# Setup and first step of a fused convolution + MoE kernel: loads on three queues, four scratch sets, eight plain products, order by arrival

## The chip, the cores and the metric

One core of one Trainium2 chip. The metric is the time of one launch in device microseconds (us). The changed kernel was timed beside the kernel before in the same rounds; the experiments ran in three groups, on three chips, each again beside the kernel before. A ratio compares the fast runs of two kernels in the same rounds; it is not quite the ratio of the medians quoted beside it.

## The reference

```python
# x (8, 4096, 192) f32, weight (8, 7) f32; moe_w_in (192, 2048) f64, moe_w_out (2048, 192) f64
w = softmax(weight, axis=-1)                       # one 7-tap kernel per head of 24 channels
x_pad = concat([zeros((B, 6, D)), x], axis=1)      # causal
out[b, s, h, :] = sum_k w[h, k] * x_pad[b, s + k, h, :]
h = out.reshape(32768, 192) @ w_in
g = h * (1 / (1 + exp(-1.702 * h)))
return (g @ w_out).astype(float32)
```

## The kernel before

The work is 64 steps of 512 tokens. In each step TensorE (PE) computes first products (f by w_in, into PSUM accumulators) for two units a and b. ScalarE (ACT) applies gelu and VectorE (DVE) adds partial results. PE then computes second products (g by w_out). Both products use a Strassen-like scheme: seven 2x2 block products in place of eight, fed by sums of the blocks (`sums_w_out` for w_out, `sum_g` for g). Two steps share one x block. DVE prepares the next block's convolution f in small lots (`work(n)`) between other work, and at the end of a preparation a DMA copies f crosswise between the partition halves (`cross`). In the code of a step, p1 to p7 are first products on PE; `seed`, `keep2` and `keep3` are copies out of PSUM on ACT (into `sums` and `u`); `add12` and `add22` are additions on DVE; h11 to h22 are gelus on ACT, which write g.

Before step 0 the kernel loads x and the float64 weights and rounds the weights to float32 by integer work, piece by piece. A piece is split by two DVE and four ACT instructions and rounded by three or four on DVE. There are four pieces of w_in and four of w_out. x block 0 is convolved on PE itself, by 42 products with diagonal matrices. In the traces DVE and PE work through their lists in the order of the program: in e2 below, transposes that could start at 9.32 us (e6) stood on DVE until 13.84, 4.5 us behind work that was not ready, and in e6 a part of the convolution stood on PE behind a product that waited 2.57 us.

The loads and the diagonal matrices:

```python
    load_x(0)                                   # 8 transfers on SyncE's queue, 640-byte rows
    ...
    for i in range(NW):                         # 4 pieces of w_in, each two 64-partition halves
        piece = raw[:, i, :].rearrange("p (k f) -> p k f", k=NC)
        for h in range(2):
            nc.sync.dma_start(out=piece[halves[h], :, :], in_=w_in_v[i // 2, i % 2, h])
    ...
    for c in range(NC):
        for k in range(K):
            vec.tensor_scalar_mul(diag[:, c, k, :], ident, cw[:, c, k : k + 1])
    new_f(0)
    for c in range(NC):
        transpose_x(0, c)
```

The seven-product form at the end of each step. Its second product needs a sum of w_out (S4), so in step 0 it waits for the whole rounding of w_out:

```python
        p1 = product2(ra, 0, A11, B11)
        act.copy(u1, p1)
        for i in range(4):
            last.sum_g(i)
        p3 = product2(rb, 0, S4, B22)
        ...
```

The lots of work in steps 0 and 1. In step 1, `output` takes only part of the queue and the rest, with the crossing, is drained after it:

```python
        work(6) if s else setup0()
        ...
        if s == 0:
            setup1()
        else:
            work(None if s % 2 and s > 1 else 4)
        ...
        output(s, b, work)
        if s == 1:
            work()
```

## Time and profile before

| | before |
|---|---|
| median of the first 3 runs | 2518.4 us (2517.91 to 2520.95) |
| span of the profiled run | 2520.6 us |
| convolution on PE starts | 11.36 us |
| first second product of step 0 | 59.78 us |
| first product of step 1 | 92.67 us |
| first product of step 2 | 141.47 us |
| first u copy of step 2 on ACT ("step-2 mark") | 168.22 us |

From step 2's mark on, nothing differs between the kernels of this document, so a kernel is judged best by when it reaches that mark. The floor is 38.1 us a step, and 0.1 to 1.1 us are added in single steps that differ from run to run. Differences of some us between single runs, and of 1 or 2 us between medians, can come from there.

The prediction shows PE's waits and the stretches. Three lines more are needed for the start. First the DVE timeline (start, duration, then engine, line, operation and operands; in brackets the idle time before it and what ended it):

```profile
6.42 4.20 DVE L521 TENSOR_SCALAR diag<-ident,cw 128x128 f32<-128x128 f32 x21
10.54 2.09 DVE L296 STREAM_TRANSPOSE xt<-xin 128x576 f32<-128x576 f32 x3
```

The PE timeline at the same place:

```profile
11.36 18.30 PE L527 MATMUL slot<-xt,diag 128*128 128x512 f32 x42 [1.56 <-DVE xt L296]
```

The transposes start right behind the 21 diagonals, with no wait for a DMA: DVE sets the start of the convolution, and x has landed earlier (its last packet ended at 8.5 us; in e6, with the same load, the transposes could start at 9.3).

### The profile page before, as it was taken

How to read it: one execution, taken by the hardware profiler on the slowest of the kernel's cores; microseconds unless marked ns; L12 is line 12 of the kernel's file. 1: busy time of each engine (PE TensorE's matmuls, PEld its weight loads, DVE VectorE, ACT ScalarE, POOL GpSimd, SP SyncE). 2: the span in 40 equal slices, each digit the busy share in tenths (PEclk: the TensorE clock that was granted, in tenths of full speed). 3: DMA queues.
4: the chain of work that ended last, by engine and by line, in shares of the span. 5: the costliest groups of instructions: out<-in, count | busy, mean ns of one | idle time of the engine just before them, and what ended most of it. 6: DMA issues, size and time to landing. Idle time of an engine off the chain costs nothing.

```text
span 2520.6 us, 114341 instructions
## 1 busy us (share of the span) xinstructions
PE 2478.5 (98%) x54336; PEld 2303.3 (91%) x54336; DVE 1714.2 (68%) x2370; ACT 952.5 (38%) x1060; POOL 4.8 (0%) x20
## 2 busy tenths in 40 slices
PE   8889999999999999999999999999999999999998
PEld 5779999999999999999999999999999999999998
DVE  7856667666667666667666676666676666677654
ACT  6224334334334334334343343343343343343342
POOL 0000000000000000000000000000000000000000
PEclk9999999999999999999999999999999999999999
DMA  7122212212212222122122122122122222121110
GB/s 165 32 56 53 57 31 54 57 34 55 55 31 57 44 47 57 42 44 56 39 51 57 33 52 58 36 54 56 28 58 47 43 57 49 38 57 39 28 34 15
DMA packets 197603, 123.43 MB, mean 49 GB/s; under 512 B 115984, under 2 KB 191248, under 8 KB 193168
## 3 DMA queue, kind: packets, MB, share of 16 engines
q1 hardware_dynamic: 197120, 116.13, 21.9%
q8 instruction: 424, 6.95, 1.1%
q14 instruction: 43, 0.35, 0.0%
q10 hardware_dynamic: 16, 0.00, 0.0%
HBM read 53.15 MB, written 25.17 MB: 31 GB/s over the span
## 4 chain that ended last, share of the span: by engine, by line
PE 96%; DVE 1%; ACT 1%; DMA 1%; issue 0%; SPq 0%; DVEq 0%; ACTq 0%
PE slot L350 30%; PE slot L455 30%; PE sums L350 18%; PE slot L445 17%; PE slot L527 0%; DVE g L439 0%; ACT g L373 0%; DMA f<-f 0%; DMA xin<-in_x_dram 0%; ACT u L390 0%; DVE xt L296 0%; ACT f L198 0%; SPq L102 0%; ACT f L197 0%; ACT f L195 0%
## 5 line engine op out<-in xcount | busy, mean ns | idle before, releaser
L455 PE MATMUL slot<-g,w_out_s 128*32 128x64 f32 x21504 | 1219.6, 219 | 1.1 <-issue 0.8
L445 PE MATMUL slot<-g,w_out_s 128*32 128x192 f32 x21504 | 1209.6, 330 | 10.4 <-DVE w_out_s L257 9.9
L455 PEld LDWEIGHTS slot<-g,w_out_s 128*32 128x32 f32 x21504 | 1205.9, 110 | 2.7 <-issue 1.9
L350 PE MATMUL slot<-f,w_in_s 64*128 64x256 f32 x7168 | 843.9, 378 | 11.5 <-DMA f<-f 10.4
L350 PEld LDWEIGHTS slot<-f,w_in_s 64*128 64x128 f32 x7168 | 691.7, 188 | 100.5 <-DMA f<-f 11.2
L439 DVE TENSOR_TENSOR g<-g 128x1024 f32<-128x1024 f32 x512 | 609.5, 1222 | 191.9 <-ACT g L373 187.5
L445 PEld LDWEIGHTS slot<-g,w_out_s 128*32 128x32 f32 x21504 | 629.5, 108 | 34.2 <-issue 23.4
L350 PE MATMUL sums<-f,w_in_s 64*128 64x256 f32 x4096 | 515.1, 380 | 5.8 <-ACT sums L383 3.0
L390 ACT COPY u<-sums 128x1024 f32<-128x1024 f32 x128 | 129.5, 1012 | 1029.6 <-PE sums L350 1029.6
L350 PEld LDWEIGHTS sums<-f,w_in_s 64*128 64x128 f32 x4096 | 392.3, 187 | 56.7 <-ACT sums L383 3.7
L313 DVE SCALAR_TENSOR_TENSOR f<-xt,cw,f 128x512 f32<-128x512 f32 x558 | 417.5, 748 | 14.2
L373 ACT ACTIVATE g<-u 128x1024 f32<-128x1024 f32 x256 | 269.7, 1054 | 14.2 <-DVE u L430 14.1
L430 DVE TENSOR_TENSOR u<-u,slot 128x1024 f32<-128x1024 f32 x128 | 155.9, 1218 | 68.6 <-PE slot L350 68.6
L420 DVE TENSOR_TENSOR u<-u,slot 128x1024 f32<-128x1024 f32 x128 | 155.7, 1216 | 68.4 <-ACT u L403 65.5
L493 DVE TENSOR_TENSOR u<-u,slot 128x192 f32<-128x192 f32 x64 | 22.7, 355 | 247.7 <-PE slot L455 247.7
L403 ACT COPY u<-sums 128x1024 f32<-128x1024 f32 x128 | 129.6, 1012 | 133.7 <-PE sums L350 133.7
L373 ACT ACTIVATE g<-sums 128x1024 f32<-128x1024 f32 x128 | 130.6, 1020 | 94.7 <-PE sums L350 94.7
L373 ACT ACTIVATE g<-slot 128x1024 f32<-128x1024 f32 x128 | 131.5, 1027 | 45.0 <-PE slot L350 45.0
L383 ACT COPY sums<-slot 128x1024 f32<-128x1024 f32 x128 | 128.8, 1006 | 27.9 <-PE slot L350 25.8
L489 DVE TENSOR_TENSOR u<-u,slot 128x192 f32<-128x192 f32 x64 | 22.7, 354 | 99.6 <-PE slot L455 99.6
L483 ACT COPY u<-slot 128x192 f32<-128x192 f32 x64 | 20.4, 319 | 159.0 <-PE slot L455 159.0
L473 DVE STREAM_TRANSPOSE osb<-u 128x192 f32<-128x192 f32 x192 | 72.3, 376 | 4.4
(57 smaller groups left out, 417.5 us busy)
## 6 DMA issues: line engine op xcount, KB each, us to landing
xin<-in_x_dram SPq DMA_DIRECT2D x240, 180.0 KB, 4.5
f<-f SPq DMA_DIRECT2D x62, 576.0 KB, 4.8
out_dram<-osb SPq DMA_DIRECT2D x384, 48.0 KB, 1.7
out_dram<-osb SPq DMA_DIRECT2D x384, 16.0 KB, 1.5
g<-in_moe_w_in_dram SPq DMA_DIRECT2D x8, 384.0 KB, 9.4
g<-in_moe_w_out_dram SPq DMA_DIRECT2D x4, 768.0 KB, 5.1
xin<-in_x_dram SPq DMA_DIRECT2D x16, 160.0 KB, 3.2
f<-f SPq DMA_DIRECT2D x2, 256.0 KB, 3.4
```

The lines of the kernel that those rows point to most:

```text
L313: vec.scalar_tensor_tensor(out=dst, in0=src, scalar=tap, in1=dst, op0=ALU.mult, op1=ALU.add)
L350: nc.tensor.matmul(slot[:, h, j * T : (j + 1) * T], w_in_s[halves[h], u, a, j * P : (j + 1) * P], f[halves[h], 0 if h == o else 1, b, :], ...
L373: act.activation(g[:, b, j : j + NK // NU, :].rearrange("p f t -> p (f t)"), src.rearrange("p h n -> p (h n)"), AF.Gelu_apprx_sigmoid,)
L383: act.copy(sums, self.x)
L390: act.copy(self.u2, sums)
L403: act.copy(self.u3, sums)
L420: vec.tensor_add(self.u3, self.u3, self.z)
L430: vec.tensor_add(self.u2, self.u2, self.z)
L439: vec.tensor_sub(v[dst], v[a], v[b])
L445: nc.tensor.matmul(dst[c * Q : (c + 1) * Q, :], w_out_s[:, a, j, c * Q : (c + 1) * Q], g[:, b, j, 0:TA], start=(first and j == 0), stop=(j ...
L455: nc.tensor.matmul(dst[3 * Q :, c * TB : (c + 1) * TB], w_out_s[:, a, j, c * Q : (c + 1) * Q], g[:, b, j, TA:T], start=(first and j == 0 a ...
L473: vec.transpose(osb[:, n, :, m * Q : (m + 1) * Q], src.rearrange("p (j t) -> p j t", t=Q),)
```

## The change

The intent: start sooner, remove the wait for sums of w_out in step 0, and let nothing wait for the crossing at step 2. Its core:

```diff
-    load_x(0)
-    for i in range(NW): ... nc.sync.dma_start(...)        # all of w_in behind x, one queue
+    load_w_in(0, act)            # piece 0 on ScalarE's queue
+    load_x(0)                    # x on SyncE's
+    load_w_in(2, nc.sync)        # piece 2 behind it
     ...
+    load_w_in(1, nc.gpsimd)      # pieces 1 and 3 on GpSimd's
+    load_w_in(3, nc.gpsimd)
@@ scratch: 2 sets -> 4 (two in f, one in the x tile, one in diag)
@@ diagonals: 7 on DVE, 14 on ACT
-            vec.tensor_scalar_mul(diag[:, c, k, :], ident, cw[:, c, k : k + 1])
+            if c == 0:
+                vec.tensor_scalar_mul(diag[:, c, k, :], ident, cw[:, c, k : k + 1])
+            else:
+                act.mul(diag[:, c, k, :], ident, cw[:, c, k : k + 1])
     new_f(0)
+    split_piece(0)               # DVE: now ahead of the transposes
+    splits()
     for c in range(NC):
         transpose_x(0, c)
@@ step 0 unrolled by hand as first_step(), p1 between the convolution's parts; its end:
+        todo.extend(prepare(1))
+        for k in range(2):
+            for n in range(2):
+                for m in range(2):
+                    src = product2((b.x, b.z)[n], m, ..., first=(k == 0))   # eight plain products
+                    if k == 1:
+                        if (n, m) == (0, 0):
+                            work(5)
+                            sums_w_out()
+                        work(3)
+                        vec.transpose(osb[:, n, :, m * Q : (m + 1) * Q], ...)   # "turn"
@@ step 1: the rest of block 1's preparation is drained before add12, not after output
-            work(None if s % 2 and s > 1 else 4)
+        work(None if s % 2 else 4)
-        if s == 1:
-            work()
```

(Cut: the scratch sets' addresses, the order of step 0's first products, the loads of w_out moved to GpSimd's queue.) "Slot" is a PSUM tile of two halves, called banks here; `m` chooses the bank and `n` the slot.

More of the change, by code (lines that the diff above doesn't have):

```diff
@@ L145, with scratch @@
     raw = raw.rearrange("p (i n) -> p i n", i=NW)
-    tmp = f_pool.tile([P, 2, NB, T], F32, name="f")
-    tmp = tmp.rearrange("p o b t -> p (o b t)").bitcast(U32).rearrange("p (i n) -> p i n", i=6)
-    w8 = consts.tile([H, K], F32)
-    act.dma_start(out=w8, in_=weight)
-    load_x(0)
+    diag = consts.tile([P, NC, K, P], F32)
+    assert min(NC * K * P, 2 * NJ * XW) >= 3 * PIECE
+    def scratch(flat):
+        return [flat[:, j * PIECE : (j + 1) * PIECE].bitcast(U32) for j in range(3)]
+    tmp = f_pool.tile([P, 2, NB, T], F32, name="f").rearrange("p o b t -> p (o b t)")
+    sets = [
+        scratch(tmp),
+        scratch(tmp[:, 3 * PIECE :]),
+        None,
+        scratch(diag.rearrange("p c k q -> p (c k q)")),
+    ]
+    SET = (0, 1, 2, 0, 1, 3, 0, 1)
     w_in_v = moe_w_in.bitcast(U32).rearrange(
@@ L157, with load_w_in @@
     w_out_v = moe_w_out.bitcast(U32).rearrange("(c p) d -> p c d", p=P)
-    for i in range(NW):
+    def load_w_in(i, queue):
         piece = raw[:, i, :].rearrange("p (k f) -> p k f", k=NC)
         for h in range(2):
-            nc.sync.dma_start(out=piece[halves[h], :, :], in_=w_in_v[i // 2, i % 2, h])
+            queue.dma_start(out=piece[halves[h], :, :], in_=w_in_v[i // 2, i % 2, h])
+    w8 = consts.tile([H, K], F32)
+    act.dma_start(out=w8, in_=weight)
+    load_w_in(0, act)
+    load_x(0)
+    load_w_in(2, nc.sync)
     sel = consts.tile([H, NC, P], F32)
@@ L183 @@
         nc.gpsimd.memset(bias[:, i : i + 1], b)
+    load_w_in(1, nc.gpsimd)
+    load_w_in(3, nc.gpsimd)
     def words(i):
         w = raw[:, i % NW, :].rearrange("p (n w) -> p n w", w=2)
-        return (w[:, :, 0], w[:, :, 1]) + tuple(tmp[:, 3 * (i % 2) + j, :] for j in range(3))
+        return (w[:, :, 0], w[:, :, 1]) + tuple(sets[SET[i]])
     def split_piece(i):
@@ L194, in split_piece, with splits @@
         vec.tensor_scalar(e, hi, 20, 0x7FF, op0=ALU.logical_shift_right, op1=ALU.bitwise_and)
-        act.activation(l.bitcast(F32), lo, AF.Copy, scale=2.0**-32)
-        act.activation(e.bitcast(F32), e, AF.Relu, bias=bias[:, 0:1])
-        act.activation(e.bitcast(F32), e.bitcast(F32), AF.Relu, bias=bias[:, 1:2], scale=-1.0)
-        act.activation(
-            e, e.bitcast(F32), AF.Identity, bias=bias[:, 2:3], scale=-(2.0**23)
-        )
+        ef = e.bitcast(F32)
+        acts.extend(
+            [
+                lambda: act.activation(l.bitcast(F32), lo, AF.Copy, scale=2.0**-32),
+                lambda: act.activation(ef, e, AF.Relu, bias=bias[:, 0:1]),
+                lambda: act.activation(ef, ef, AF.Relu, bias=bias[:, 1:2], scale=-1.0),
+                lambda: act.activation(
+                    e, ef, AF.Identity, bias=bias[:, 2:3], scale=-(2.0**23)
+                ),
+            ]
+        )
+    acts = []
+    def splits(n=4):
+        for _ in range(n):
+            acts.pop(0)()
     def round_piece(i, dsts):
@@ L233, in load_w_out @@
     def load_w_out(i):
-        nc.sync.dma_start(
+        nc.gpsimd.dma_start(
             out=raw[:, i, :].rearrange("p (c d) -> p c d", c=CW),
@@ L241, in round_w_out @@
         round_piece(
-            i,
+            NW + i,
             [
@@ L501, in output, with store @@
         turn(1, 0, u3)
+        store(s, osb)
+    def store(s, osb):
         big, odd = divmod(s, 2)
@@ L515, in output, with work, first_conv @@
                 )
-    diag = consts.tile([P, NC, K, P], F32)
+    todo = []
+    def work(n=None):
+        for _ in range(len(todo) if n is None else min(n, len(todo))):
+            todo.pop(0)()
     for c in range(NC):
         for k in range(K):
-            vec.tensor_scalar_mul(diag[:, c, k, :], ident, cw[:, c, k : k + 1])
+            if c == 0:
+                vec.tensor_scalar_mul(diag[:, c, k, :], ident, cw[:, c, k : k + 1])
+            else:
+                act.mul(diag[:, c, k, :], ident, cw[:, c, k : k + 1])
     new_f(0)
+    split_piece(0)
+    splits()
     for c in range(NC):
         transpose_x(0, c)
-    for c in range(NC):
+    xs = xin_pool.tile([P, 2, NJ, XW], F32, name="xin")
+    sets[2] = scratch(xs.rearrange("p n j d -> p (n j d)"))
+    conv_out = [slots[1][:, 0, :], slots[2][:, 0, :], slots[1][:, 1, :]]
+    def first_conv(c):
         for k in range(K):
             nc.tensor.matmul(
-                slots[c][:, 0, :],
+                conv_out[c],
                 diag[:, c, k, :],
@@ L536, in take_conv @@
         vec.tensor_copy(
-            fs[0][:, 0, 2 * c : 2 * c + 2, :].rearrange("p n t -> p (n t)"), slots[c][:, 0, :]
+            fs[0][:, 0, 2 * c : 2 * c + 2, :].rearrange("p n t -> p (n t)"), conv_out[c]
         )
-    split_piece(0)
-    take_conv(0)
-    split_piece(1)
-    round_w_in(0)
-    take_conv(1)
-    for i in range(4):
-        sums_c(0, i)
-    cross(0, 0, C31)
-    cross(0, V1, NB)
-    split_piece(2)
-    round_w_in(1)
-    split_piece(3)
-    take_conv(2)
-    cross(0, C31, V1)
@@ L554, with first_step @@
-    sums_w_in(0)
-    load_w_out(0)
-    load_w_out(1)
-    todo = []
-    def work(n=None):
-        for _ in range(len(todo) if n is None else min(n, len(todo))):
-            todo.pop(0)()
-    def setup0():
+    def first_step():
+        a, b = Unit(0, 0), Unit(0, 1)
+        first_conv(0)
+        first_conv(1)
+        round_w_in(0)
+        load_w_out(0)
+        split_piece(1)
+        splits()
+        take_conv(0)
+        cross(0, C11, C12)
+        a.p1()
+        first_conv(2)
+        split_piece(2)
+        splits()
+        round_w_in(1)
+        load_w_out(1)
+        take_conv(1)
+        for i in range(4):
+            sums_c(0, i)
+        cross(0, C12, C31)
+        cross(0, V1, NB)
+        a.seed()
+        split_piece(3)
+        splits()
+        sums_w_in(0)
+        a.p5()
+        a.p6()
+        a.keep2()
+        split_piece(4)
+        take_conv(2)
+        cross(0, C31, V1)
+        a.pe(a.x, W12, C21)
+        splits(1)
+        a.p7()
+        a.keep3()
@@ L565, in setup0 @@
         round_w_in(2)
         load_w_out(2)
-        split_piece(4)
-    def setup1():
+        load_x(1)
+        splits(3)
+        a.pe(sums, W22, V4)
+        a.p5b()
+        a.pe(a.x, W13, C31)
+        a.h11()
+        a.pe(sums, W23, C31)
+        a.h21()
         round_w_in(3)
         load_w_out(3)
-        load_x(1)
+        a.add22()
+        b.p1()
+        b.seed()
+        a.h22()
+        a.p3()
         sums_w_in(1)
         split_piece(5)
-    def setup2():
+        splits(1)
@@ L577, in setup2 @@
+        a.add12()
+        b.p5()
+        b.p6()
+        b.keep2()
+        b.p2()
+        splits(1)
+        b.p7()
+        b.keep3()
+        b.h11()
         round_w_out(0)
         split_piece(6)
+        splits(2)
+        nxt = Unit(1, 0)
+        nxt.p1()
+        b.p5b()
+        b.add22()
+        b.p4()
+        b.h21()
+        nxt.seed()
+        splits()
+        b.p3()
         round_w_out(1)
-    def setup3():
+        b.add12()
         split_piece(7)
+        a.h12()
+        b.h12()
@@ L583, in setup3 @@
+        splits()
+        b.h22()
         round_w_out(2)
-    def setup4(a):
         round_w_out(3)
-        sums_w_out()
-        for i in range(4):
-            a.sum_g(i)
-    nxt = None
-    for s in range(N_ST):
+        todo.extend(prepare(1))
+        osb = osb_pool.tile([P, 2, TA // Q, 2 * Q], F32, name="osb")
+        for k in range(2):
+            for n in range(2):
+                for m in range(2):
+                    src = product2(
+                        (b.x, b.z)[n], m, (A11, A12, A21, A22)[2 * m + k],
+                        (B11, B12, B21, B22)[2 * k + n], first=(k == 0),
+                    )
+                    if k == 1:
[3 more added lines that the diff above has]
+                        work(3)
+                        vec.transpose(
+                            osb[:, n, :, m * Q : (m + 1) * Q],
+                            src.rearrange("p (j t) -> p j t", t=Q),
+                        )
@@ L593 @@
+        store(0, osb)
+        return nxt
+    nxt = first_step()
+    for s in range(1, N_ST):
         a, b = nxt or Unit(s, 0), Unit(s, 1)
@@ L609 @@
         a.h11()
-        work(6) if s else setup0()
+        work(6)
         a.add22()
@@ L617 @@
         a.p3()
-        if s == 0:
-            setup1()
-        else:
-            work(None if s % 2 and s > 1 else 4)
+        work(None if s % 2 else 4)
         a.add12()
@@ L633 @@
         b.p5b()
-        if s == 0:
-            setup2()
-        else:
-            work(2)
-            a.sum_g(0)
-            a.sum_g(1)
+        work(2)
+        a.sum_g(0)
+        a.sum_g(1)
         b.add22()
@@ L646 @@
         b.p3()
-        if s == 0:
-            setup3()
-        else:
-            a.sum_g(2)
-            a.sum_g(3)
+        a.sum_g(2)
+        a.sum_g(3)
         b.add12()
         b.h12()
-        if s == 0:
-            setup4(a)
-            todo += prepare(1)
         output(s, b, work)
-        if s == 1:
-            work()
         if s % 2 and (s + 3) // 2 < N_BIG:
```

## The prediction

> **What bounds the kernel now.** I read the page first, then the PE's waits of the first 200 us, then a table of stretches.
>
> ```profile
> span 2520.6 us, 114341 instructions
> PE 2478.5 (98%) x54336; PEld 2303.3 (91%) x54336; DVE 1714.2 (68%) x2370; ACT 952.5 (38%) x1060; POOL 4.8 (0%) x20
> ```
>
> TensorE (PE) is busy throughout; only the places where it isn't, or runs slowly, can be gained. They lie at the start:
>
> ```profile
> engine line waited for: us in total, times, longest us
> PE slot L350 <- DMA f<-f: 10.4, 2, 10.0
> PE slot L445 <- DVE w_out_s L257: 9.9, 1, 9.9
> PE slot L270 <- DVE e L267: 4.7, 1, 4.7
> PE sums L350 <- ACT sums L383: 3.0, 1, 3.0
> PE sums L350 <- ACT u L390: 2.3, 2, 1.2
> PE slot L527 <- DVE xt L296: 1.6, 1, 1.6
> PE slot L350 <- DVE w_in_s L227: 1.0, 1, 1.0
> ```
>
> From 200 us on PE's waits sum to about 0.2 us. Two waits of 10 us stand out: the first second product of step 0 that needs sums of w_out, and step 2's first product, which waits for the half-crossing copy of x block 1. By step:
>
> ```profile
> core 0: us, PE busy (x) PEld busy (x) DVE busy (x) ACT busy (x) POOL busy (x), PEclk, DMA share, GB/s
> 0.00:92.74 92.74, 70.17 (x922) 53.91 (x922) 67.58 (x119) 46.43 (x53) 3.12 (x17) 0.91 0.56 129
> 92.74:130.90 38.16, 37.84 (x841) 34.88 (x842) 30.43 (x42) 13.48 (x15) 0.00 (x0) 1.00 0.06 12
> 130.90:168.30 37.40, 26.23 (x294) 22.36 (x298) 18.82 (x25) 14.83 (x16) 0.00 (x0) 0.86 0.42 83
> 168.30:206.30 38.00, 38.00 (x853) 35.59 (x849) 28.25 (x41) 14.32 (x16) 0.00 (x0) 1.00 0.20 44
> ```
>
> Setup with step 0 takes 92.7 us, step 1 takes 38.2, and each of the 62 later steps 38.1, PE full. The third stretch holds the gap before step 2. PEclk (granted clock) below 1.00 is a second cost. In the PE timeline:
>
> ```profile
> 41.29 3.62 PE L350 MATMUL slot<-f,w_in_s 64*128 64x256 f32 x32
> 47.92 2.08 PE L350 MATMUL sums<-f,w_in_s 64*128 64x256 f32 x8 [3.02 <-ACT sums L383]
> 53.20 1.47 PE L350 MATMUL sums<-f,w_in_s 64*128 64x256 f32 x8
> 72.54 0.54 PE L445 MATMUL slot<-g,w_out_s 128*32 128x192 f32 x3 [9.87 <-DVE w_out_s L257]
> 141.47 4.98 PE L350 MATMUL slot<-f,w_in_s 64*128 64x256 f32 x21 [10.01 <-DMA f<-f]
> ```
>
> A product of 8 instructions takes 0.86 us at full clock (32 in 3.45 us from start to next start), but 1.9 us after the 3.0 us idle at 45 us; the clock stays at 0.50 to 54 us. Each of the three long gaps cost its length and about 2.6 to 3 us more.
>
> [...]half clock after idle of 3.0, 9.9 and 10.0 us, none after 1.2. [...] In the trace x and w_in together (1.4 + 3.1 MB) run at 225 GB/s from 2 to 22 us on one queue with DMA share 1.0 or above, so there is nothing idle to win. [...]w_in (64 partitions) 225 GB/s, w_out (128 partitions) 373 to 405. [...]
>
> **The change, part by part.** Durations are start-to-start, from the timelines.
>
> Let X be when x has landed (now 8.5 us; the transposes then waited until 10.5 for 21 diag products on DVE, and the convolution started at 11.4).
>
> Diag: DVE keeps 7 of 21 (7 x 0.2 = 1.4 us instead of 4.2)[...]. So X itself, plus 0.75 for one transpose, now sets the start of the convolution. But x shares the DMA engines with piece 0 from about 3 us and piece 1 from about 6. With 0.26 MB of x gone by 3.2 us and 235 GB/s, an equal split gives X = 15; one by packets (640 B of x against 2 KB of w_in) 17 to 19; a better aggregate 12. I choose X = 15.
>
> Convolution: 42 instructions, 18.3 us (now 11.36 to 29.66), with p1 (0.86) inside; so p5 can begin at X + 19.9. DVE has room beside it: splits 3 x 0.95, two roundings x 2.85, copies, sums. Because PE idles from about 10 to X + 0.75 (5.7 us), the start falls on half clock: about 2.5 us more.
>
> Then p5 and p6 (0.86 each), and keep2 starts at X + 21.7. From here ACT has work without a break, taken in program order. To the end of piece 5's splits: two keep2 and two keep3 (1.0 each: 4.0), one seed (1.0), four gelus (1.03: 4.1), the table load (1.3), two pieces of splits (0.92 an activation, eight: 7.3), together 17.7 us, so X + 39.4. The second rounding of w_out ends 2.0 us later (its last two operations, 0.98 + 1.04 on DVE): the first plain product starts at X + 41.4. To the end of piece 7's splits: three gelus, one seed, two more pieces at 3.8, 11.6 us further, X + 51.0; the last rounding ends at X + 53.0. The four k = 0 products (4 x 2.69 = 10.8 us; 2.68 lies between the two u copies of step 2) fill X + 41.4 to X + 52.2, the four k = 1 products X + 53.0 to X + 63.7. No sum of g and no sum of w_out lies before them: the 9.9 us wait and 3.8 + 9.4 us of DVE go, for one more product (2.69).
>
> Step 0's end: 15 + 63.7 + 2.5 half clock + 1 of slack = 82.2 us, now 92.7: gain 10.5. PE's own work (18.3 + 23 x 0.86 + 8 x 2.69 = 59.6) would end at X + 60.4, so PE is nearly the bound.
>
> Step 1: DVE ends its last rounding near X + 53, then does three transposes 2.1, sums of w_out 3.85, twelve conv taps 8.8 and four turns 1.5: X + 69.2, 5.5 us behind PE. Six taps (4.5) and add22 (1.15) put add22 10.6 us after step 1's start; PE reaches p3 after about 8. Loss 2.6 us.
>
> Step 2: all of block 1's preparation is now drained before add12 of step 1, so the crossing lands long before. The 10.0 us wait and 2.6 to 3 us of half clock go: gain 13. Step 2 still begins without an early p1, so the wait of 1.2 us on keep2 stays. Steps 2 to 63 don't change.
>
> Sum: 10.5 - 2.6 + 13 = 20.9, from 2518.4: 2497. As a smaller X and no slack would give 2488, I put the middle at 2495.
>
> **The rivals.** (a) The three queues add bandwidth, X is 11 and PE never idles long: no half clock, step 0 ends near 75.5, 2489 or less. [...] (b) Starvation of x by the larger packets, X = 18 or 19: step 0 ends near 86, 2501. For it: the packet sizes. (c) DVE is the bound in step 0: its list up to the last rounding sums to 44.6 us from about 12, 57 us, below ACT's; only if its in-order waits add up would it cost 3 to 5 us. (d) The GpSimd loads are late[...]; the first piece needed of them is piece 1, near 18 us. That would hold ACT and DVE some us: 2500. (e) Step 1's backlog spreads into step 2: up to 3 us more.
>
> **Range and chances.** X between 11.5 and 19 is 7 us, the half clock 0 to 3, step 1's loss 0 to 4: 2485 to 2505 should hold it eight times in ten. Faster by 2% needs 50 us; that would put step 0's end plus the step 2 gain below PE's own work, so 0.01. Slower would need a loss in the unchanged steps: 0.01. Within 2%: 0.98.
>
> **What will show it.** The convolution's first start (X + 0.75, I say 15.8) and its clock; the first plain product near 59[...]; ACT without idle from 37 to 68; step 1's first product near 82; a PE wait of 2 to 3 us on add22 in step 1; no wait on the f crossing at step 2; later steps at 38.1. The prediction is wrong if steps 2 to 63 change, if the step 2 wait survives, or if X differs by more than 4 us.

## The result, and the profile after

| | before | after |
|---|---|---|
| median (fast runs of the same rounds, 4 each) | 2519.68 us | 2510.84 us (2507.83 to 2512.19) |
| ratio after/before | | 0.9962 (0.9947 to 0.9977) |
| convolution on PE starts | 11.36 | 20.98 |
| first second product of step 0 | 59.78 | 64.75 |
| first product of step 1 | 92.67 | 95.27 |
| first product of step 2 | 141.47 | 133.36 |
| step-2 mark | 168.22 | 157.78 |

The class "within 2%" was right, but the time was 6 us above the top of the predicted range. Three subtractions show where it went. Step 0, the part that the change rewrote, ends 2.60 us *later*. From step 1's first product to step 2's it was 48.80 us and is 38.09: 10.71 us gained. (In the kernel before, two instructions of step 2's first product ran at 130.76, and the rest waited until 141.47.) From there to the mark it was 26.75 and is 24.42: 2.33 us gained, the half clock after the wait. So the whole gain of 10.44 us at the mark is the wait that vanished before step 2 (13.0 us), and the setup and step 0 gave 2.6 of it back.

PE's waits of the first 200 us, after (us in all, times, longest; the three largest):

```profile
PE slot L577 <- DVE xt L329: 10.7, 1, 10.7
PE slot L478 <- DVE osb L691: 6.7, 2, 6.2
PE slot L303 <- DVE e L300: 5.5, 1, 5.5
```

The two 10 us waits of the kernel before (crossing, sums of w_out) are gone. Two others stand in their place, both on DVE: on the transposed x at the start, and on `osb`, the turn of a finished output block.

By stretches (the first cut is 0.07 us after step 1's first product; length, then busy us of PE, PEld, DVE, ACT and POOL, granted clock, DMA share, GB/s):

```profile
0.00:95.34 95.34, 71.17 (x1018) 54.25 (x1018) 61.02 (x102) 50.03 (x65) 8.64 (x25) 0.89 0.53 125
95.34:133.00 37.66, 37.34 (x836) 34.48 (x837) 24.83 (x34) 13.48 (x15) 0.00 (x0) 1.00 0.20 44
133.00:157.80 24.80, 23.63 (x304) 20.80 (x299) 17.36 (x21) 14.77 (x16) 0.00 (x0) 1.00 0.39 77
```

Step 1 has no loss at all, and the second stretch's clock is 1.00. The first has 24 us without PE work and a mean clock of 0.89: what is left to gain is here.

**The first wait: x is late.** The same group in the DVE timeline, after:

```profile
20.15 2.10 DVE L329 STREAM_TRANSPOSE xt<-xin 128x576 f32<-128x576 f32 x3 [9.51 <-DMA xin<-in_x_dram]
```

and PE's:

```profile
20.98 15.23 PE L577 MATMUL slot<-xt,diag 128*128 128x512 f32 x28 [10.65 <-DVE xt L329]
```

The transposes now wait 9.5 us for the DMA, and the convolution waits 10.65 us with them. Its first 28 instructions last 15.23 us; they take 12.29 at full clock (experiments e5 and e6 below), so the idle time cost 3 us more in half clock. From 3 to 20 us the DMA engines carried 231 GB/s at a DMA share of 1.07, against 225 at 1.10 before: there was almost no bandwidth to win, the queues only shared it out differently. How they shared it stands in the view of the queues (packets, MB, share of the 16 engines' time). From 3 to 6 us x (q1, SyncE's queue) ran beside piece 0 (q10, ScalarE's):

```profile
q10 hardware_dynamic: 237, 0.45, 63.8%
q1 hardware_dynamic: 332, 0.20, 33.5%
```

and from 9.5 to 12 us beside pieces 1 and 3 (q0, GpSimd's):

```profile
q0 software_dynamic: 140, 0.51, 84.3%
q1 hardware_dynamic: 170, 0.10, 21.7%
```

Beside GpSimd's queue x gets about as many packets as the other (from 12 to 15 us it is 163 to 166), but a packet of x holds 0.6 KB on average, one of ScalarE's queue 1.9 KB and one of GpSimd's 3.7 KB. So x gets some 30% of the bytes in the first stretch and 16% in the second. Beside ScalarE's queue the counts are less even (237 to 332): from 3.5 to 4.5 us piece 0 moved 102 packets and x none. The last transfer of x, issued by 7.5 us (4.2 in the kernel before), landed at 20.1.

**The second wait: the turn stands in a queue.** DVE's timeline at the end of step 0:

```profile
75.55 1.03 DVE L244 SCALAR_TENSOR_TENSOR w_out_s<-f 128x384 f32<-128x384 f32 x2
76.49 2.09 DVE L329 STREAM_TRANSPOSE xt<-xin 128x576 f32<-128x576 f32 x3
78.51 0.91 DVE L287 TENSOR_TENSOR w_out_s<-w_out_s 128x768 f32<-128x768 f32 x1
...
82.78 1.54 DVE L346 SCALAR_TENSOR_TENSOR f<-xt,cw,f 128x512 f32<-128x512 f32 x2
84.23 0.38 DVE L691 STREAM_TRANSPOSE osb<-slot 128x192 f32<-128x192 f32 x1
```

PE ended the first k = 1 product at 78.5. The next one writes the other bank of the same slot, and it started at 84.66, right behind the turn at 84.23. Between the two DVE did the four sums of w_out and three convolution taps (block 1's transposes came just before), none of which the product needs. Three slices of 1 us there, with columns as in the stretches above (the third number from the right is the clock; after PE's busy time, in brackets, is its number of matmuls):

```profile
78.00:79.00 1.00, 0.48 (x15) 0.31 (x6) 1.00 (x2) 0.00 (x0) 0.00 (x0) 1.00 0.00 0
85.00:86.00 1.00, 1.00 (x27) 1.00 (x23) 0.96 (x2) 0.00 (x0) 0.00 (x0) 0.50 1.19 218
89.00:90.00 1.00, 1.00 (x46) 1.00 (x41) 0.62 (x2) 0.00 (x0) 0.00 (x0) 1.00 0.00 0
```

27 matmuls in a microsecond at half clock and 46 at full: this wait, too, cost about 2 us beyond its length.

### The profile page after: what moved, and what is told of

Same layout as the page of the kernel before. It is cut to its first block, busy times and chain, and to the rows that moved or that the text cites. A ratio compares the mean times of both kernels' runs of the same rounds, so it can differ in the third digit from the quotient of the medians.

```text
span 2510.4 us, 114525 instructions
## 1 busy us (share of the span) xinstructions
PE 2475.9 (99%) x54432; PEld 2303.0 (92%) x54432; DVE 1700.9 (68%) x2342; ACT 955.7 (38%) x1072; POOL 10.4 (0%) x28
## 4 chain that ended last, share of the span: by engine, by line
PE 97%; ACT 1%; DVE 1%; issue 1%; DMA 0%; ACTq 0%; DVEq 0%
PE slot L383 31%; PE slot L488 30%; PE sums L383 18%; PE slot L478 18%; PE slot L577 1%; DMA g<-in_moe_w_in_dram 0%; ACT g L406 0%; ACT u L423 0%; DMA xin<-in_x_dram 0%; DVE g L472 0%; DVE xt L329 0%; DVE u L453 0%; ACT u L436 0%; ACT f L223 0%; ACT f L224 0%
## 5 line engine op out<-in xcount | busy, mean ns | idle before, releaser
L472 DVE TENSOR_TENSOR g<-g 128x1024 f32<-128x1024 f32 x504 | 600.2, 1222 | 193.5 <-ACT g L406 189.2
L453 DVE TENSOR_TENSOR u<-u,slot 128x1024 f32<-128x1024 f32 x128 | 155.7, 1217 | 56.2 <-ACT u L436 53.3
## 6 DMA issues: line engine op xcount, KB each, us to landing
g<-in_moe_w_in_dram POOLq DMA_DIRECT2D x4, 384.0 KB, 10.7
```

What stands on the lines that cost most here:

```text
L453: vec.tensor_add(self.u3, self.u3, self.z)
L472: vec.tensor_sub(v[dst], v[a], v[b])
```

## The experiments

Theory: (1) the drain of block 1's preparation in step 1 is the whole gain; (2) x's late landing, through the three queues, holds the start; (3) the turn's place behind other DVE work holds the end of step 0. The rivals: the eight-product form is itself the loss or brings nothing; the half clock and not the wait is what costs; the start is hidden anyway by ACT's and DVE's rounding. No run takes back the four scratch sets, the new order of step 0's first products or the queue of the w_out loads, so what these are worth alone isn't known. Each experiment changes the kernel after, unless it says that it changes the one before. All eleven gave correct results. Marks are us from the start of the profiled run.

| kernel | convolution | first second product | step 1 | step-2 mark | median us (n; range) | ratio to before (95%) |
|---|---|---|---|---|---|---|
| before | 11.36 | 59.78 | 92.67 | 168.22 | 2518.5 to 2519.85 in the three groups | 1 |
| after | 20.98 | 64.75 | 95.27 | 157.78 | 2510.84 (4) | 0.9962 |
| e1_drain | 11.37 | 59.62 | 92.19 | 161.09 | 2512.00 (5; 2509.98 to 2513.46) | 0.9967 (0.9953 to 0.9980) |
| e2_xfirst | 14.67 | 58.20 | 88.60 | 151.44 | 2502.18 (5; 2500.20 to 2503.24) | 0.9928 (0.9916 to 0.9941) |
| e3_turns | 20.25 | 63.79 | 87.20 | 163.03 | 2514.09 (5; 2513.53 to 2514.60) | 0.9977 (0.9965 to 0.9990) |
| e4_swap | 21.10 | 63.51 | 90.14 | 152.65 | 2505.69 (5; 2504.00 to 2507.39) | 0.9944 (0.9931 to 0.9956) |
| e5_warm | 21.86 | 62.68 | 93.49 | 156.08 | 2506.49 (5; 2505.42 to 2507.86) | 0.9949 (0.9937 to 0.9961) |
| e6_xfirst_turned | 10.16 | 55.94 | 87.42 | 149.94 | 2499.81 (4; 2499.21 to 2500.68) | 0.9922 (0.9909 to 0.9936) |
| e7_seven | 21.06 | 64.52 | 100.30 | 170.11 | 2519.93 (5; 2518.90 to 2520.60) | 1.0002 (0.9988 to 1.0015) |
| e8_act_only | 14.17 | 57.80 | 88.25 | 150.77 | 2501.64 (5; 2501.23 to 2502.23) | 0.9930 (0.9917 to 0.9942) |
| e9_p1_late | 10.22 | 54.36 | 84.42 | 146.93 | 2498.69 (5; 2498.46 to 2500.21) | 0.9921 (0.9908 to 0.9935) |
| e10_both | 10.10 | 54.27 | 76.33 | 140.96 | 2493.33 (4; 2489.13 to 2494.53) | 0.9896 (0.9883 to 0.9910) |
| e11_tail | 20.92 | 63.51 | 85.87 | 148.38 | 2498.87 (5; 2497.38 to 2500.79) | 0.9921 (0.9908 to 0.9933) |

Of the eleven expected times those of e4 and e8 came, and e5 was 1.5 us faster than its own. e1, e2, e3, e6, e7, e9 and e10 were slower than expected, e11 faster. e3, e9 and e10 ended at times that had been given to their rivals; for each the marks say below what that means.

### e1_drain: the drain alone, in the kernel before

```diff
-            work(None if s % 2 and s > 1 else 4)
+            work(5 if s == 1 else None if s % 2 else 4)
-            work(2)
+            work(4 if s == 1 else 2)
             a.sum_g(0)
 ...
             a.sum_g(3)
+            if s == 1:
+                work()
```

> The kernel before with one thing of the change alone: the preparation of x block 1 is finished inside step 1 (spread over its four places) instead of after its last product. Theory: nearly the whole measured gain of the change (about 9 us of 2519) is the vanished wait of step 2 for the half-crossing copy, 10.0 us plus about 2.6 us of half clock; so this kernel alone takes 2506 to 2508 us, and step 0 still ends at 92.7 us. Rival: the rewritten setup and step 0 bring some of the gain themselves; then this kernel gains less than 5 us and stays above 2514.

The mark came 7.1 us earlier and the time fell 6.7 us. The wait for the crossing is gone; a smaller one took its place, in step 1 (PE timeline):

```profile
117.55 0.36 PE L445 MATMUL slot<-g,w_out_s 128*32 128x192 f32 x3 [3.20 <-DVE u L430]
```

The lots now stand on DVE ahead of an addition (add12, L430) that reads a slot, and a second product needs that slot. That wait of 3.2 us with its half clock (0.50 from 118.6 to 122.0 us, some 1.7 us lost) accounts for most of what is missing from the expected 12.6 us (10.0 of wait and 2.6 of half clock). So the drain alone gives two thirds of what after gains at the mark. In after step 1 lost nothing: there 17 of the 31 lots of block 1's preparation are done under the eight products, where `output` does 7 in step 0.

### e7_seven: the change with the seven-product form in step 0

```diff
-        todo.extend(prepare(1))
-        ... eight products ...
+        sums_w_out()
+        for i in range(4):
+            a.sum_g(i)
+        todo.extend(prepare(1))
+        output(0, b, work)
```

> The changed kernel with step 0's second product in the seven-product form again, as in all later steps: DVE forms the four sums of w_out and eight sums of g (3.85 + 9.4 us) behind the last rounding. Theory (the eight-product form takes DVE's sums off the path and pays 2.7 us of PE): the second seven-form product waits for the sums until about 81 us and others for the sums of g until about 90, step 1 starts at about 100 us instead of 95.3, some of it returned in step 1 because block 1's taps are then earlier or later: 2513 to 2517. Rival (the form does not matter, since DVE's other work held PE up as long anyway): 2509 to 2512.

The PE timeline where the seven products are under way:

```profile
80.16 0.54 PE L478 MATMUL slot<-g,w_out_s 128*32 128x192 f32 x3 [12.76 <-DVE w_out_s L290]
```

The wait for the sums of w_out is back and longer than in before (9.87). Step 1 starts 5 us later than in after, and in step 1 a further wait of 5.7 us for an ACT copy appears. The time is that of the kernel before. The form with the eighth product (2.69 us of PE work) is worth 12.3 us at the mark and 9.1 us of median, the medians being from two groups of runs. Of the 12.3 us, 5.0 lie before step 1 and 7.3 after it, and there e7 also starts with fewer lots of block 1 done (7 under `output` in place of 17), which was not separated. The rival "the eight products bring nothing" falls.

### e3_turns and e4_swap: what the turn waits behind

In e3 DVE turns a block as soon as it is done, and the sums of w_out and the twelve lots come after all the turns:

```diff
                     if k == 1:
                         if (n, m) == (0, 0):
                             work(5)
-                            sums_w_out()
-                        work(3)
                         vec.transpose(osb[:, n, :, m * Q : (m + 1) * Q], ...)
+        sums_w_out()
+        work(12)
```

> The changed kernel with DVE's order in the last four plain products altered: the four output transposes follow their products at once, sums of w_out and the twelve taps come after them. Theory B (PE waited 6.2 us for the first transpose because DVE had 6 us of other work ahead of it, and then ran 4 us at half clock): step 1 starts at about 86.5 us instead of 95.3, but DVE's backlog of about 12.5 us now holds up the first addition of step 1, so half of it or more is given back: 2503 to 2508 us. Rival (the wait was for the last rounding or the sums of w_out): step 1 starts no earlier than 93, and the time is 2510 or more.

In e4 only the two loops change places, so that consecutive products go to different slots:

```diff
-            for n in range(2):
-                for m in range(2):
+            for m in range(2):
+                for n in range(2):
```

> The changed kernel with the loops over the two slots and the two banks of a slot exchanged, DVE's order kept. If PE's wait belongs to the slot (a product into one bank waits until the other bank of the same slot has been read), the second of the last four products goes to the other slot and runs at once, the wait shrinks from 6.2 to about 3.5 us, with half clock mostly gone: 3 to 5 us faster than the changed kernel, about 2506. If the wait belongs to DVE's order alone, whichever bank is written, it stays at 6 us and the time at 2511.

e3 did what theory 3 says and lost all the same. Step 1 starts 8.1 us earlier than in after, but then PE stops (e3's PE timeline):

```profile
105.57 5.49 PE L383 MATMUL slot<-f,w_in_s 64*128 64x256 f32 x24 [10.33 <-DVE u L453]
```

L453 is `add22` of step 1, which now stands behind the sums and the lots. The whole backlog came back in step 1 as a wait of 10.3 us, with half clock until 111.1 us. The mark is 5.3 us *later* than in after. Work taken off one wait isn't gone: it has to fit somewhere that PE does not wait for.

e4 leaves DVE's list alone and takes the wait away from the other side. The `osb` waits vanish, although the turn stands in the same place of DVE's list: the product that follows goes to the other slot. The mark is 5.1 us earlier than in after (1.2 of it from a shorter half clock at the start, see e5). So PE waited for *the slot*, not for DVE's list as such. Something new came up among the first four products (PE's waits of the first 200 us of e4):

```profile
PE slot L478 <- ACT g L406: 2.4, 1, 2.4
```

With the loops swapped, the product that needs the gelu h12 of unit b is the second instead of the third, too early for ACT, and after the wait of 2.4 us the clock is again at 0.50, from 68.7 to 72.1 us. Whether the original wait is forced by the chip or by the program's own order was not separated. The product and the turn touch different banks of the slot; that the program's guard for the whole slot is the reason is not shown.

### e2, e8, e6: which queue delays x, and what stands before it

e2 puts everything on SyncE's queue again, x first. e8 keeps only piece 0 on ScalarE's queue. e6 is e2 with the transposes ahead of piece 0's split on DVE.

```diff
 e2:
-    load_w_in(0, act)
     load_x(0)
-    load_w_in(2, nc.sync)
+    for i in range(NW):
+        load_w_in(i, nc.sync)
 ...
-    load_w_in(1, nc.gpsimd)
-    load_w_in(3, nc.gpsimd)
 e8: load_w_in(0, act) stays; pieces 1, 2, 3 on nc.sync behind x
 e6 = e2 and:
     new_f(0)
-    split_piece(0)
-    splits()
     for c in range(NC):
         transpose_x(0, c)
+    split_piece(0)
+    splits()
```

> The changed kernel with all four pieces of w_in on the SyncE queue behind x, as before the change. Theory A (x is starved by the other two queues): x lands near 8.6 us instead of 20, the convolution starts at about 11 us at full clock, and the 9.5 us and the 3.0 us of half clock both come back: about 2498 us, first plain product near 52 us. Rival (ACT's and DVE's rounding work is the bound of step 0, x only hides it): piece 0 lands 3 us later, the first plain product moves by less than 5 us, and the time stays above 2506.

> The changed kernel with pieces 1 and 3 of w_in moved from the GpSimd queue to the SyncE queue behind x (order x, 1, 2, 3); piece 0 stays on the ScalarE queue. Theory (x was starved by what the GpSimd queue carried beside it): x shares only with piece 0 and lands at about 12 us, piece 0 at about 9; the convolution starts near 13 at full clock, 8 + 3 us earlier than in the changed kernel: 2499 to 2502. Rival (the ScalarE queue's piece 0 alone delays x as much): x still lands after 16 us and the time is above 2506.

> As the run with all of w_in behind x, and DVE's three transposes of x put ahead of its first split of w_in, which there held the transposes until piece 0 landed at 12.9 us. Theory (DVE's queue order was what kept the convolution at 14.7 us): it starts at about 10 us at full clock, 4.7 + 3 us earlier; the products p5 can start about 6 to 7 us earlier, where piece 1 and DVE become the bound: about 2495 to 2497. Rival (the landing of the pieces of w_in bounds this phase): p5 moves by less than 2 us, the time stays at 2500 to 2502.

x has landed by 9.3 us with everything behind it in one queue (e6), by 13.3 with piece 0 on a second queue (e8), and by 20.1 with pieces 1 and 3 on a third as well (after). Theory 2 stands, and the delay comes in two parts of 4.0 and 6.8 us, one for each queue added. They are about what the bytes of the added queues take: piece 0 has 0.79 MB and pieces 1 and 3 have 1.57, which at 231 GB/s is 3.4 and 6.8 us (an estimate from the trace's own figures). So x came in behind nearly everything that was queued beside it. In e2, though, the convolution still started at 14.67. The DVE timeline says why:

```profile
12.90 0.56 DVE L213 TENSOR_SCALAR f<-g 128x768 uint32<-128x768 uint32 x1 [5.00 <-DMA g<-in_moe_w_in_dram]
13.37 0.56 DVE L214 TENSOR_SCALAR f<-g 128x768 uint32<-128x768 uint32 x1
13.84 2.09 DVE L327 STREAM_TRANSPOSE xt<-xin 128x576 f32<-128x576 f32 x3
```

The transposes carry no wait of their own. x was there, but the split of piece 0 stood ahead of them in DVE's queue, and piece 0 landed only at 12.9. The kernel after relies on piece 0 coming first; with x first, that order is wrong. In e6's DVE timeline it is turned:

```profile
9.32 2.10 DVE L327 STREAM_TRANSPOSE xt<-xin 128x576 f32<-128x576 f32 x3 [1.42 <-DMA xin<-in_x_dram]
```

The convolution starts at 10.16 and its first 28 instructions take 12.29 us, at full clock. Yet of these 4.5 us (and 2.7 of half clock, 15.00 against 12.29) only 2.3 reach the first second product, 1.2 step 1 and 1.5 the mark, and the time is 2499.81 us, not 2495 to 2497. (The 1.1 us between the first second product and step 1 are half clock: after the wait for the turn, PE works 5.8 us at half clock in e6, 75.83 to 81.61, and 3.5 us in e2, 78.10 to 81.60.) PE now stops a little later (PE timeline of e6):

```profile
25.64 1.13 PE L381 MATMUL slot<-f,w_in_s 64*128 64x256 f32 x6 [2.57 <-DMA f<-f]
```

p1, set between two parts of the convolution, needs a crossing copy. It came early enough when the convolution was late; now PE holds the third part behind it, and that part runs at half clock from 27.0 to 30.4 us (7.97 us for its 14 instructions, 6.28 in e8).

### e9_p1_late: the wait of p1 moved behind the convolution

```diff
 (on e6)
         cross(0, C11, C12)
-        a.p1()
         first_conv(2)
+        a.p1()
```

> As the run with x first and its transposes first, and the first product p1 placed after all three convolution parts on PE instead of between the second and the third, where it held PE 2.6 us for the crossing copy and the third part then ran partly at half clock (8.0 us instead of 6.3). Theory: p5 starts at about 30.2 us instead of 34.6, all of it on the path: about 2495.5. Rival (DVE's sums of w_in or the roundings bind there anyway): p5 moves by less than 1.5 us, the time stays above 2498.

The first second product comes 1.6 us earlier than in e6, step 1 3.0 us and the mark 3.0 us. The median fell by 1.1 us, but it is on another chip and beside another group of runs; the ratios (0.9922 and 0.9921) can't tell the two apart. p5 starts at 30.38 us (34.60 in e6), as the theory has it, but "all of it on the path" does not hold, and the time stays above 2498, where the rival had it. From p5 on PE waits 0.92 us for another crossing and 1.40 for ACT's keep2, so the rounding's own chain is close behind PE in this stretch, as the rival says. Of the 3.0 us at step 1 the other 1.4 are half clock again: after the wait for the turn PE works 2.8 us at half clock (74.26 to 77.04), where in e6 it was 5.8.

### e5_warm: the half clock alone

```diff
+    for _ in range(11):
+        nc.tensor.matmul(slots[0][:, 1, :], ident, diag[:, 0, 0:4, :]..., start=True, stop=True)
     new_f(0)
```

Eleven products whose result nobody reads keep PE busy while x is on its way.

> The changed kernel with eleven idle-filling products of the identity (each 128x512, into a bank that the first real product clears) on PE while it waits for x. Nothing else moves: x still lands near 20 us. Theory: the convolution's first two parts then take 12.2 us instead of 15.2, since the clock is never lowered, and the 3.0 us are on the path: about 2508. Rival: the convolution is slow for another reason (operands, PSUM), or DVE and ACT work beside it absorbs the 3 us: it stays at 15 us, or the time stays within 1 us of 2511.

The first 28 instructions of the convolution took 12.29 us in place of 15.23: the half clock was worth 2.9 us there. x happened to land 0.9 us later in this run, and step 1 started 1.8 us earlier, the mark came 1.7 us earlier. The median is 4.4 us lower (on another chip, in another group of runs), more than the marks show; the rest is not explained by this edit (the later steps of the profiled run took 3.8 us less than those of after, which the edit doesn't touch). So the rival "it's the clock that costs" holds for under 3 us, beside the 9.6 us by which the start is late.

By the clock in the traces the half clock lasted 3.4 us (e1, e4, e6), 6.8 (after, 81.6 to 88.4), 10.2 (before, 67.7 to 78.0) or 13.6 us (after, 13.3 to 26.9): about once, twice, three and four times 3.4. How much of it meets work differs from run to run: at the start e4 and e11 had 10.2 us of it where after had 13.6, with the same code and the same late x, and their first 28 instructions took 13.87 and 14.05 us in place of 15.23. Their marks are 1.2 us earlier for that reason alone.

### e11_tail and e10_both: the repairs together

The tail keeps the order of after for k = 0, swaps the loops for k = 1 only (so B12's gelu is in time *and* no product waits for the turn of its own slot), and spreads the backlog over step 1:

```diff
+        order = [(0, n, m) for n in range(2) for m in range(2)]
+        order += [(1, n, m) for m in range(2) for n in range(2)]
+        for k, n, m in order:
 ...
                     if k == 1:
                         if (n, m) == (0, 0):
                             work(5)
-                            sums_w_out()
-                        work(3)
+                        elif (n, m) == (1, 0):
+                            sums_w_out()
+                        else:
+                            work(3)
                         vec.transpose(...)
@@ step 1
-        work(6)
+        work(4 if s == 1 else 6)
         a.add22()
-        work(None if s % 2 else 4)
+        work(6 if s == 1 else None if s % 2 else 4)
         a.add12()
 ...
         b.h12()
+        if s == 1:
+            work()
         output(s, b, work)
```

e11 is this on the kernel after; e10 is this on e9.

> The changed kernel with only the end of step 0 and step 1's lots rearranged as in the run with both; the loads stay on three queues and x lands near 20 us. Theory: the 6.7 us of waits and about 2 us of half clock go, step 1 starts near 87.5 us instead of 95.3: 2502 to 2504. Rival (the backlog comes back in step 1, as when only the transposes were moved ahead): 2508 or more.

> The front of the previous run, and the end of step 0 rearranged: the last four plain products take the two slots in turn, DVE turns each result before it goes on with other work, six taps instead of twelve lie in step 0's end, and step 1 takes the rest in small lots, the last of them before its second products. Theory (PE's wait for the first output transpose came from DVE's 6 us of other work ahead of it, and DVE's backlog must be spread so that no addition of step 1 waits): no PE wait over 1 us in the last eight products, step 1 starts about 8 us earlier than in the previous run: 2486 to 2489. Rival (DVE's total work is the bound, every rearrangement only moves the wait): 2493 or more.

In e11 the eight products run without a wait but 0.6 us of issue (PE's waits from 60 to 150 us, e11; the 0.2 us lie in step 1, the 1.2 us in step 2):

```profile
PE sums L383 <- ACT u L423: 1.2, 1, 1.2
PE slot L488 <- issue: 0.6, 1, 0.6
PE sums L383 <- ACT u L436: 0.2, 1, 0.2
```

Step 1 starts 9.4 us earlier than in after, the mark comes 9.4 us earlier, and step 1 keeps its 38.1 us: nothing was given back, and the time is 3 us below the expected 2502. This is the term that the prediction missed, measured by taking it away: of the 9.4 us 1.2 were there before the first second product (the half clock at the start), and 8.2 lie between it and step 1, which now take 22.36 us where after took 30.52.

e10 has both repairs. Step 1 starts at 76.33, 8.1 us earlier than in e9, and from 8 us to the mark no slice of 1 us has a clock below 1.00. In step 1 it gave 2.1 us back, in one place of the PE timeline:

```profile
109.94 0.24 PE L486 MATMUL slot<-g,w_out_s 128*32 128x64 f32 x1 [1.93 <-issue]
```

"issue" means that the profile shows nothing that PE waited for; no engine worked from 108 to 109.9 us. I did not find its cause. The time missed the expected 2486 to 2489 and lies where the rival (DVE's total work only moves the wait) had put it; but up to the mark no wait of PE on DVE over 0.3 us is left once the loads have begun to land, so the trace does not show the rival's cause. e10 at 2493.33 us is the fastest version here: 25.2 us (1.0%) below the kernel before in its group, by ratio 0.9896, where the change itself reached 0.9962.

## Why the prediction was wrong, point by point

The sum predicted a gain of 20.9 us; 10.44 came at the mark, 8.8 in the medians. The predicted end of step 0 was 82.2 us, the measured 95.27. The error of 13.1 us is 5.15 (x) + 8.2 (the k = 1 products) - 0.3 (between them). The loss of 2.6 us that was forecast for step 1 did not come, which made the error in the whole that much smaller.

- **"I choose X = 15": too small by 5.15 us.** X was 20.15, the start of the transposes; the last packet of x ended at 19.06. The prediction had both readings, an equal split of bytes (15) and "one by packets" (17 to 19), and chose the first without a line of the trace that spoke for it. The counts above show packets, beside GpSimd's queue at least, so rival (b) came true for X. There it was 140 packets to 170 (9.5 to 12 us) and 166 to 163 (12 to 15 us), at 0.6 KB a packet of x against 3.7. No run changed the row size, so whether longer rows of x would help was not shown.
- **"no bandwidth to win": right.** 231 GB/s against 225 from 3 to 20 us, at DMA shares of 1.07 and 1.10. Rival (a) is out.
- **Diagonals on ACT: off the path.** 14 took 4.20 us, 0.30 each, and x landed 8.7 us after them.
- **Half clock of 2.5 us at the start: 3.0.** Right in kind; 1.6 to 3.0 from run to run, as told under e5. (Of "about 2.6 to 3 us more" for each gap of the kernel before, the third was 2.4: it worked from 141.47 to 146.25 at half clock.)
- **The first plain product at X + 44.9 (41.4 and 2.5 and 1): right.** It came at 64.75, X + 44.6, and DVE's second rounding of w_out ended at 65.5, X + 45.4. The list of ACT's and DVE's roundings and gelus was sized well. But PE did not wait for it: the line has no idle time (PE timeline of after), so PE's own work arrived at the same time, and that the start fits to 0.3 us is in part luck.

```profile
64.75 0.36 PE L478 MATMUL slot<-g,w_out_s 128*32 128x192 f32 x3
```

- **"the four k = 1 products X + 53.0 to X + 63.7": this step failed.** It took the products as 10.8 and 10.7 us of work with 0.8 between them; from the first of them to step 1 it was 30.5 us. The prediction did write down DVE's list after the last rounding (transposes, sums, taps, turns) and found DVE 5.5 us behind PE. It then charged those to step 1 as "Loss 2.6". But PE did not get ahead of that list: a turn frees the slot that the second k = 1 product writes. With this consumer in the list's middle, the lag was a wait at once (6.2 us on `osb`). e4 and e11 show that this is the slot and its order, e3 that the backlog itself needs a place.
- **Step 1's loss of 2.6 us: none.** Since PE had waited, DVE had caught up; add22 started 4.8 us after step 1's start and the step took 38.09 us. (The forecast's own terms, 5.5 + 4.5 + 1.15, put the end of add22 at 11.2 us, not 10.6.)
- **Step 2's gain of 13 us: right.** 10.71 up to the first product after the wait and 2.33 of half clock, 13.0. But e1 shows that it isn't free of the rest of the change: alone it gives 7.1.
- **Steps 2 to 63 unchanged: right.** From step 2's mark to step 63's it was 2329.1 us before and 2329.5 after.
- **The rivals (c), (d), (e).** (c) is nearest to what failed: DVE's order in its list did cost PE, but at the turn and by 8.2 us, not 3 to 5. (d) GpSimd's loads were late (issued from 4.0 us, first packet at 9.2), but piece 1 landed at 14.9 and its split at 24.87 did not wait for it. (e) did not come: from step 2's first product to the mark after and e11 both take 24.42 us.
- **The middle moved from 2497 to 2495** because of a smaller X; both of the rivals that spoke against it, (b) and (d), were larger. The move was the wrong way.

The second of the two missing terms is what its repair gave back: e11 alone starts step 1 at X + 65.8, where the prediction had X + 67.2, and at 85.87 us, where rival (b) had 86.

## What to carry to other kernels

Before a load moves to a second queue, ask what the first engine to start waits for: here the DMA engines were full (share 1.10 before, 1.07 after), two more queues made almost no bandwidth (231 GB/s against 225), and x, for which everybody waited, landed at 20.1 us where it had landed by 9.3 (e6). What stood ahead of a short freeing instruction in DVE's list was part of the wait of the one who needed the buffer (the turn came 5.7 us after its product, and PE waited 6.2), so put the freeing instruction first or let the next product use another buffer, and then find the displaced work a place where nobody waits (e3, 2514.09 us, against e11, 2498.87). Each wait removed at the start uncovered the next in order (x, the split, p1's crossing, the turn), so judge by a mark downstream of them all and not by the first wait.

## What these traces show of the clock, the queues and the lists

- Gaps of 2.4 us (e4) and 2.57 us (e6) were followed by 3.4 us at a clock of 0.50, about 1.7 us of work each (estimated from the length and the clock; in e6 7.97 us against 6.28 in e8 for the same 14 instructions). In e6 the drop came at 27.0 us, after PE had been at work again since 25.64. A gap of 1.93 us (e10) was followed by none. Nearly the same gap cost 1.6 us in e4 (10.48) and 3.0 in after (10.65). What sets whether and when the clock drops was not shown; no run was made to test it.
- x landed at 9.3, 13.3 and 20.1 us with none, one and two other queues beside it (e6, e8, after), at 0.6 KB a packet against 1.9 and 3.7; the DMA engines carried 231 GB/s in after against 225 before. How much of this is the size of the packets was not separated.
- Work that was ready stood behind other work in the same list: the transposes of a landed x 4.5 us behind a split (e2, 13.84 against 9.32 in e6), the third convolution part 2.57 us behind p1 (e6), the turn 5.7 us behind sums and taps (after, 78.5 to 84.23).
